# Two batches of the transposed mixer output end to end in one ring tile, so that chunks across a batch border are read in one piece

## Chip, cores and metric

One core of one Trainium2 chip. The metric is the device time of the whole kernel in microseconds (us), lower is better.

## The reference, cut to what matters

A frequency filter mixes each batch along the sequence; a feed-forward part with a leaky ReLU follows, over all tokens.

```python
x: (8, 3008, 256)   w_in: (256, 2048)   w_out: (2048, 256)
y = irfft(rfft(x, axis=1) * (filt_r + 1j * filt_i), n=3008, axis=1)
t = y.reshape(8 * 3008, 256)                # 24064 tokens
h = t @ w_in
out = maximum(0.01 * h, h) @ w_out
```

24064 tokens are 47 chunks of 512. A batch has 3008 tokens, 5.875 chunks, so each of the 7 inner batch borders falls inside a chunk.

## The kernel before

The mixer writes each batch, transposed, into one of two tiles in turn (channels on partitions, tokens along the row, two halves `dt` of 128 channels). The first product of the feed-forward part reads chunks of 512 tokens from there.

```python
yts = [cpool.tile([P, NDT, N], FP16, name=f"yt{i}") for i in range(2)]
...
def sb_group(b, g, copy):                     # last step of the mixer
    dt, h = g // 8, g % 8
    def go():
        ...                                   # 4 matmuls into a PSUM bank
        yv = yts[b % 2][:, dt, :].rearrange("p (a c) -> p a c", c=N2)
        copy(yv[:, :, ds(4 * h, 4)], ps.rearrange("p c a -> p a c"))     # L246
    return go
...
def moe1_group(ci, g):                        # first product of chunk ci, 8 groups
    ...
    pieces, t = [], ci * CH
    while t < (ci + 1) * CH:                  # cut at every batch border
        e = min((ci + 1) * CH, (t // N + 1) * N)
        pieces.append((t // N, t % N, t - ci * CH, e - t))
        t = e
    for j in range(2):
        ct = 2 * g + j
        for b, lo, o, ln in pieces:
            for dt in range(NDT):
                nc.tensor.matmul(ph[:, j, ds(o, ln)], w_in_sb[:, dt, ts(ct, P)],   # L376
                                 yts[b % 2][:, dt, ds(lo, ln)],
                                 start=(dt == 0), stop=(dt == NDT - 1))
    nc.scalar.activation(gts[ci][:, ds(2 * g, 2), :], ph, AF.Lrelu)      # L381

def moe2_slice(ci, g):                        # second product, 8 matmuls of 256 columns: L390
    ...
    nc.scalar.copy(ost[:, tj % 2, :], po)     # every second slice: L397
...
for slot in range(SL * (NCHUNK + 1)):         # a chunk is 8 slots
    ci, g = divmod(slot, SL)
    if ci < NCHUNK:
        moe1_group(ci, g)
    for f in tasks.get(slot, ()):             # steps of the mixer for a later batch
        f()
    if ci > 0:
        moe2_slice(ci - 1, g)
```

Ahead of the slots stands a start of some 42 us: warm-up matmuls, the loads, and the mixer of batch 0. From the first matmul of L376 on I call it the main stage.

## Time and profile before

| | before |
|---|---|
| whole run, 3 runs | 783.31 us median (783.25 to 783.39) |
| span of the profiled run | 782.1 us (a fourth run, of 783.91 us) |
| TensorE busy | 99% |
| start, up to the first matmul of L376 | 42.48 us |
| matmuls of L376 | 1728 |

The page gives each engine's busy time, the chain of waits and the groups of instructions. The lines are in the prediction.

### The profile page before, as it was taken

What the parts mean: (1) busy time and instruction counts of PE and PEld (TensorE: products, weight loads), DVE (VectorE), ACT (ScalarE), POOL (GpSimd) and SP (SyncE); (2) the same over time, 40 slices, a digit from 0 to 9 for tenths busy, and PEclk for the clock granted to TensorE, in tenths of its full rate; (3) what the DMA queues carried; (4) which work ended last, traced back from release to release, by engine and by line L of the source; (5) the groups of instructions that cost most, each with busy time, mean ns of one, the idle gap of its engine ahead of it and who ended that gap; (6) DMA issues with size and microseconds to landing.
All of it is one profiled execution on the core that took longest, in us unless ns stands there. A gap on an engine that the chain in (4) does not pass through costs nothing.

```text
span 782.1 us, 13672 instructions
## 1 busy us (share of the span) xinstructions
PE 773.4 (99%) x5844; PEld 531.4 (68%) x5844; DVE 367.3 (47%) x462; ACT 551.2 (70%) x784; POOL 152.3 (19%) x126
## 2 busy tenths in 40 slices
PE   9899999999999999999999999999999999999998
PEld 4366677666776667766777667776677666776666
DVE  3879751865237641577307754087432765200000
ACT  3686769676787767777587775967668776666664
POOL 5963300340004300052001510025000340000000
PEclk9999999999999999999999999999999999999999
DMA  9963102301041101510105010140101001101111
GB/s 179 226 110 73 38 28 56 94 27 42 28 108 41 41 28 41 108 42 28 42 28 121 28 37 32 42 107 28 41 28 41 28 28 41 41 33 35 41 41 54
DMA packets 39387, 44.16 MB, mean 56 GB/s; under 512 B 11266, under 2 KB 37506, under 8 KB 38658
## 3 DMA queue, kind: packets, MB, share of 16 engines
q0 software_dynamic: 13136, 17.78, 13.3%
q1 hardware_dynamic: 26192, 25.53, 9.3%
q8 instruction: 45, 0.74, 0.4%
q14 instruction: 14, 0.11, 0.0%
HBM read 35.67 MB, written 24.64 MB: 77 GB/s over the span
## 4 chain that ended last, share of the span: by engine, by line
PE 94%; DMA 2%; POOL 2%; ACT 1%; DVE 1%; issue 1%; POOLq 0%
PE ph L376 41%; PE po_ps L390 41%; PE pf L176 3%; PE pf L243 2%; PE pf L231 2%; PE pf L216 2%; DMA fb_sb<-in_filt_i_dram 2%; PE pf L390 1%; POOL fy_h_c L276 1%; ACT big L187 0%; POOL x_sb L132 0%; DVE big L297 0%; ACT big L290 0%; POOL fb_sb L140 0%; ACT gt_c L381 0%
## 5 line engine op out<-in xcount | busy, mean ns | idle before, releaser
L381 ACT ACTIVATE gt_c<-ph 128x1024 f16<-128x1024 f32 x376 | 384.8, 1023 | 195.7 <-PE ph L376 194.7
L376 PE MATMUL ph<-yt,w_in_sb 128*128 128x512 f16 (+7 forms) x1728 | 386.7, 351 | 0.3
L390 PE MATMUL po_ps<-w_out_sb,gt_c 128*128 128x256 f16 x2944 | 381.4, 272 | 0.6 <-ACT ost_c_t L397 0.6
L390 PEld LDWEIGHTS <-gt_c 128*128 128x128 f16 x3008 | 290.7, 98 | 87.1 <-issue 1.9
L376 PEld LDWEIGHTS <-w_in_sb 128*128 128x128 f16 x1728 | 162.9, 98 | 94.4 <-issue 0.4
L224 POOL TENSOR_TENSOR y_b_g<-p_b_g,p_b_g 128x512 f16<-128x512 f32 x84 | 106.9, 1272 | 225.4 <-DVE p_b_g L222 225.4
L199 DVE STREAM_TRANSPOSE big<-big 128x1024 f32<-128x1024 f32 x32 | 55.9, 1847 | 126.2 <-ACT big L187 126.2
L187 ACT CAST big<-pf 128x512 f16<-128x512 f32 x186 | 106.6, 604 | 1.7 <-PE pf L256 1.7
L246 DVE CAST yt<-pf 128x376 f16<-128x376 f32 x112 | 56.3, 544 | 86.0 <-PE pf L243 86.0
L220 DVE TENSOR_TENSOR p_b_g<-pf,fa_sb 128x512 f32<-128x512 f32 x84 | 58.1, 692 | 38.1 <-PE pf L216 35.6
L397 ACT COPY ost_c_t<-po_ps 128x256 f32<-128x256 f32 x184 | 69.4, 377 | 6.6 <-PE po_ps L390 5.4
L207 DVE STREAM_TRANSPOSE big<-big 128x1024 f32<-128x1024 f32 x28 | 51.1, 1934 | 34.1 <-ACT big L187 34.1
L221 DVE TENSOR_TENSOR p_b_g<-pf,fb_sb 64x512 f32<-64x512 f32 x84 | 58.2, 692 | 1.1
L222 DVE TENSOR_TENSOR p_b_g<-pf,fb_sb 64x512 f32<-64x512 f32 x84 | 57.4, 683 | 1.1
L132 POOL DMA_DIRECT2D x_sb<-in_x_dram x12 | 6.6, 553 | 253.3 <-PE pf L176 252.5
L243 PEld LDWEIGHTS <-big 128*128 128x128 f16 x448 | 25.6, 98 | 13.2
L176 PE MATMUL pf<-x_sb,f_sb 94*128 94x256 f16 x224 | 33.9, 272 | 0.2 <-DVE yt L246 0.2
L231 PE MATMUL pf<-y_b_g,small_sb 128*128 128x512 f16 x84 | 31.8, 379 | 0.0
L216 PE MATMUL pf<-big,small_sb 128*128 128x512 f16 x84 | 31.8, 379 | 0.0
L243 PE MATMUL pf<-i_sb,big 128*128 128x94 f16 x448 | 28.6, 206 | 0.0
L176 PEld LDWEIGHTS <-f_sb 94*128 94x128 f16 x224 | 20.9, 97 | 9.1 <-issue 0.4
L318 PE MATMUL po_ps<-idle 128*128 128x512 f16 x72 | 19.5, 418 | 1.2 <-DVE one L165 1.2
(46 smaller groups left out, 158.8 us busy)
## 6 DMA issues: line engine op xcount, KB each, us to landing
out_dram<-ost_c_t SPq DMA_DIRECT2D x92, 256.0 KB, 2.1
x_sb<-in_x_dram POOLq DMA_DIRECT2D x6, 1536.0 KB, 11.4
x_sb<-in_x_dram POOLq DMA_DIRECT2D x3, 480.0 KB, 9.8
fa_sb<-in_filt_r_dram POOLq DMA_DIRECT2D x6, 192.0 KB, 10.2
fb_sb<-in_filt_i_dram POOLq DMA_DIRECT2D x6, 192.0 KB, 8.5
w_in_sb<-in_moe_w_in_dram POOLq DMA_DIRECT2D x1, 1024.0 KB, 13.0
w_out_sb<-in_moe_w_out_dram POOLq DMA_DIRECT2D x1, 1024.0 KB, 13.0
x_sb<-in_x_dram POOLq DMA_DIRECT2D x1, 1024.0 KB, 7.9
```

The costliest lines, as they stand in the source:

```text
L176: nc.tensor.matmul(ps[:, j, :], f1_sb[:N1, n2, :], x_sb[:N1, n2, :], start=True, stop=True)
L187: copy(paired(dst)[:, ds(n0, nn), ds(e0, de)], ps.rearrange("p n (e t) -> p n e t", t=2))
L220: nc.vector.tensor_tensor(p1[:], ps, fa, AL.mult)
L221: nc.vector.tensor_tensor(p2[0:64], ps[64:P], fb[64:P], AL.mult)
L222: nc.vector.tensor_tensor(p2[64:P], ps[0:64], fb[0:64], AL.mult)
L224: nc.gpsimd.tensor_tensor(y1[:], p1[:], p2[:], AL.add)
L243: nc.tensor.matmul(ps[:, j, :], src[:, dt, n2, :], i1_sb[:, n2, :], start=True, stop=True)
L246: copy(yv[:, :, ds(4 * h, 4)], ps.rearrange("p c a -> p a c"))
L376: nc.tensor.matmul(ph[:, j, ds(o, ln)], w_in_sb[:, dt, ts(ct, P)], yts[b % 2][:, dt, ds(lo, ln)], start=(dt == 0), stop=(dt == NDT - 1),)
L381: nc.scalar.activation(gts[ci][:, ds(2 * g, 2), :], ph, AF.Lrelu)
L390: nc.tensor.matmul(po, gts[ci][:, ct, ts(tj, P)], w_out_sb[:, ct, :], start=(ct == 0), stop=(ct == NCT - 1))
L397: nc.scalar.copy(ost[:, tj % 2, :], po)
```

## The change

Intent: the two tiles become the halves of one tile of twice the length. A border between an even batch and the odd one after it then has its tokens side by side, and the chunk across it needs one piece. Only where the ring wraps (borders 2, 4 and 6) does a chunk stay cut.

```diff
-    yts = [cpool.tile([P, NDT, N], FP16, name=f"yt{i}") for i in range(2)]
+    yt = cpool.tile([P, NDT, 2 * N], FP16, name="yt")
...
-            yv = yts[b % 2][:, dt, :].rearrange("p (a c) -> p a c", c=N2)
+            yv = yt[:, dt, ds((b % 2) * N, N)].rearrange("p (a c) -> p a c", c=N2)
...
-            e = min((ci + 1) * CH, (t // N + 1) * N)
-            pieces.append((t // N, t % N, t - ci * CH, e - t))
+            e = min((ci + 1) * CH, (t // (2 * N) + 1) * 2 * N)
+            pieces.append((t % (2 * N), t - ci * CH, e - t))
...
-            for b, lo, o, ln in pieces:
+            for lo, o, ln in pieces:
...
-                        yts[b % 2][:, dt, ds(lo, ln)],
+                        yt[:, dt, ds(lo, ln)],
```

(The copy of the first batch is changed like that of the others.)

More of the change, by code (lines that the diff above doesn't have):

```diff
@@ L307, in first_sb @@
                                  i1_sb[:, n2, :], start=True, stop=True)
-        yv = yts[0][:, dt, :].rearrange("p (a c) -> p a c", c=N2)
+        yv = yt[:, dt, :N].rearrange("p (a c) -> p a c", c=N2)
         copy(yv[:, :, ds(4 * h, 4)], ps.rearrange("p c a -> p a c"))
```

## The prediction

> **What bounds the kernel now.** I read the page first: engines, slices, and the chain that ended last. In the fence: busy time by engine, then the slices of TensorE and its granted clock, then the chain by engine.
>
> ```profile
> PE 773.4 (99%) x5844; PEld 531.4 (68%) x5844; DVE 367.3 (47%) x462; ACT 551.2 (70%) x784; POOL 152.3 (19%) x126
> ...
> PE   9899999999999999999999999999999999999998
> ...
> PEclk9999999999999999999999999999999999999999
> ...
> PE 94%; DMA 2%; POOL 2%; ACT 1%; DVE 1%; issue 1%; POOLq 0%
> ```
>
> TensorE is busy in every slice, at full clock, and is 94% of the chain of waits. All that the other engines do from about 42 us on lies beside it. Second, the waits of TensorE over the whole span (us in total, times, longest): if it waited anywhere in the main stage, the change could add to that or take from it.
>
> ```profile
> PE po_ps L390 <- ACT ost_c_t L397: 0.6, 3, 0.2
> PE pf L176 <- DVE yt L246: 0.2, 1, 0.2
> ```
>
> These are the only two rows from the main stage (the six others are waits of the first 43 us); together under 1 us. So the time of the main stage is the number of columns that TensorE streams, plus what each instruction costs beside its columns. Third, the groups by shape give the matmuls that the change touches: columns after the x, count, busy time, mean.
>
> ```profile
> L376 PE MATMUL ph<-yt,w_in_sb 128*128 128x512 f16 x1280 | 328.7, 379 | 0.3
> ...
> L376 PE MATMUL ph<-yt,w_in_sb 128*128 128x448 f16 x64 | 15.7, 353 | 0.0
> ...
> L376 PE MATMUL ph<-yt,w_in_sb 128*128 128x64 f16 x64 | 7.1, 193 | 0.0
> ```
>
> The reader could take 193 ns for the price of a 64-column matmul and 379 for a 512-column one, and find that a split into 448 and 64 costs 353 + 193 - 379 = 167 ns. That is the trap here: these are latencies of overlapping instructions. What counts is from start to start. So fourth, I took stretches of three whole chunks from the end of the run, where the mixer has finished and TensorE does nothing but the two products of the feed-forward part. Chunk 41 (the middle one) holds the border of batches 6 and 7; its neighbours hold none. First all instructions, then those of L376 alone (width of stretch, then busy us and count of each engine).
>
> ```profile
> 674.15:688.04 13.89, 13.89 (x98) 9.39 (x96) 0.00 (x0) 9.24 (x13) 0.00 (x0) 1.00 0.11 38
> 688.04:702.01 13.97, 13.97 (x130) 10.32 (x128) 0.00 (x0) 9.24 (x13) 0.00 (x0) 1.00 0.11 39
> 702.01:715.91 13.90, 13.90 (x98) 9.39 (x96) 0.00 (x0) 9.25 (x13) 0.00 (x0) 1.00 0.11 39
> ```
>
> ```profile
> 674.15:688.04 13.89, 8.21 (x32) 3.13 (x32) 1.00 0.11 38
> 688.04:702.01 13.97, 8.29 (x64) 4.06 (x64) 1.00 0.11 39
> 702.01:715.91 13.90, 8.21 (x32) 3.13 (x32) 1.00 0.11 39
> ```
>
> This is the change measured inside the kernel before: 64 matmuls and 64 weight loads in place of 32 and 32, for the same columns, last 13.97 instead of 13.89 us. The price of a split chunk is 0.08 us, or 0.08 / 32 = 2.5 ns per added matmul with its weight load.
>
> **What the Trainium skill says.** "TensorE: Matmul & The Clock Gate", section "Wait — 56ns, not 53.3ns?", gives start to start of warm matmuls as N / 2.4 GHz plus a fixed cost of about 2.5 ns, with a floor near 25 ns. The trace agrees: an unsplit chunk is 32 matmuls of 512 columns and 64 of 256, so 32 x 215.8 + 64 x 109.2 = 13.89 us, the first row; and the extra 2.5 ns per matmul is the step to the second. I read the single starts too: 189.1 ns after a 448-column matmul, 28.8 after a 64-column one, 215.8 after 512; the pair is 217.9. The narrowest piece is still over the floor.
> The same page, section "Back-to-back issue gap", says of sustained pairs of weight load and matmul that 512 columns take about 131 ns and 128 about 81. The trace disagrees (215.8, and 55.8 after a 128-column piece), and the measurement decides; taking 81 for 128 would make the splits look dear.
> Section "LDWEIGHTS (loading the stationary operand)" there has P / 1.2, 107 ns for 128 columns. The trace shows 98 ns for one load, yet 64-column matmuls, each with its own load, start 28.8 ns apart. So loads are hidden even there, and removing 128 of them gives nothing further.
> "Perfetto Trace Analysis", section "Identifying the Most-Contended Engine", warns that matmul busy time is a poor measure since matmuls are pipelined. It agrees: mean duration 379 ns at a spacing of 215.8.
>
> **The change part by part.**
> Removed: batches are 3008 tokens and chunks 512, so each of the 7 inner borders falls inside a chunk (5, 11, 17, 23, 29, 35, 41), at column 448, 384, 320, 256, 192, 128, 64. Each such chunk has 8 groups x 2 tiles x 2 pieces x 2 halves = 64 matmuls, not 32; 40 x 32 + 7 x 64 = 1728, the count on the page. In the ring, batches 0-1, 2-3, 4-5 and 6-7 lie end to end. The borders inside a pair (chunks 5, 17, 29, 41) are read in one piece. Those between pairs (11, 23, 35), where the ring wraps, stay split. So 4 x 32 = 128 matmuls and 128 weight loads go: 1728 to 1600. The built programs agree: 256 instructions fewer on TensorE, the same number on every other engine.
> Price: 4 x 0.08 = 0.32 us for all four. For chunks 17 and 29 (320 + 192) the starts give 135.8 + 82.6 = 218.4, 2.6 ns over 215.8, so the same 0.08 us.
> Added: nothing. The ring takes the place of two tiles of the same total size; the copies into it keep their shape and step; the matmul reads 512 neighbouring columns.
> Moved: the waits. One tile instead of two could make writes to one half wait for reads of the other. I traced each semaphore wait in the two built programs to the instruction it waits for: of 2,594 waiting places (the matmuls of one product taken together) none differs. Only the place inside the border product changes: the first matmul now needs the copies of the later batch, where the second piece did.
> On the path: all 0.32 us, since TensorE is the path in these chunks. Sum: 783.31 - 0.32 = 782.99, say **783.0 us**, a gain of 0.04%.
>
> **The rivals.**
> 1. *The merged read waits for the mixer.* Only border 1 is near: its last copy into the tile and the first product of chunk 5 are these rows (start, duration).
>
> ```profile
> 115.95 1.00 DVE L246 CAST yt<-pf 128x376 f16<-128x376 f32 x2 [1.08 <-PE pf L243]
> ...
> 117.65 1.04 PE L376 MATMUL ph<-yt,w_in_sb 128*128 128x448 f16 x8
> ```
>
> The copy ends at 116.95, 0.7 us before the product, and the merge brings the need forward by at most two 448-column starts, 0.38 us, at one place. At the other borders the slack is 7 us and more. Cost 0; if I am wrong, 0.1 to 0.3 us once, and the gain shrinks to nothing.
> 2. *ScalarE becomes the bound in three of the four chunks.* Chunks 5, 17 and 29 also carry the first stage of a later batch, and ScalarE is busy 15.79 of 17.05 us in chunk 5. Its copy out of the output bank ends 142 to 155 ns before TensorE's next write there; where TensorE does wait on it (at 94.05 and 227.35 us, say), the distance is 52, so about 90 are spare. ScalarE starts each activation when a product ends, so the lead doesn't add up: a product is only 4 x 2.5 = 10 ns shorter, and 90 goes to about 80. For it: ScalarE is nearly full. Against: the margin holds level from slot to slot. If it won, only chunk 41's 0.08 us would stay: 783.2.
> 3. *Writes serialise against reads in the one tile.* A copy would then sit between products in each of 56 mixer slots; at perhaps 0.5 us (my estimate, from the copy's 0.54) that is some 28 us, slower by 3.6%. The equal waits of the two programs rule it out.
> 4. *The split costs its latency.* 128 x 167 ns = 21 us, faster by 2.7%. The 0.08 us of chunk 41 rules it out.
>
> **Range and chances.** The three runs before lie within 0.14 us. The candidates left are 783.0 (expected), 783.2 and 783.3 (gain eaten), plus the scatter of a different build in the first 43 us, where TensorE does wait, for which I allow 0.3 us: 782.6 to 783.4. Either 2% bound is 15.7 us away and would need rival 3 or 4. Within 2%: 0.99; 0.005 on each side.
>
> **What would show it.** Right: L376 at 1600 matmuls, 1408 of them of 512 columns, 64 each of 384, 256 and 128, none of 448, 320, 192 or 64; chunk 41 at 13.89 to 13.90 us and L376 in it at 8.21; TensorE still 99% busy; its waits still these two rows and under 1 us. Wrong: a row in which L376 or L390 waits for VectorE or ScalarE in chunks 5, 17 or 29; chunk 41 unchanged at 13.97 with half the matmuls (the 2.5 ns would then not be a cost per instruction); or the copies of L246 starting later with respect to their matmuls.

## The result, and the profile after

783.37 us median of 6 runs (783.10 to 784.10), against 783.35 us for 6 runs of the kernel before (783.18 to 783.98). The ratio is 1.0001, with a 95% interval from 0.9988 to 1.0014. A ratio is the mean time of one kernel's fast runs over that of the other's of the same rounds, so it is not quite the ratio of the medians. In whole runs the forecast gain of 0.32 us is not there.

In the trace it is. First, busy time by engine on the page of the changed kernel, then its groups of L376 by shape (shape, count, busy us, mean ns):

```profile
PE 772.2 (99%) x5716; PEld 524.0 (67%) x5716; DVE 367.4 (47%) x462; ACT 551.0 (71%) x784; POOL 152.2 (19%) x126
```

```profile
L376 PE MATMUL ph<-yt,w_in_sb 128*128 128x512 f16 x1408 | 361.5, 379 | 0.3
L376 PE MATMUL ph<-yt,w_in_sb 128*128 128x384 f16 x64 | 14.8, 326 | 0.0
L376 PE MATMUL ph<-yt,w_in_sb 128*128 128x128 f16 x64 | 8.8, 219 | 0.0
L376 PE MATMUL ph<-yt,w_in_sb 128*128 128x256 f16 x64 | 8.3, 273 | 0.0
```

There are 128 matmuls and 128 weight loads fewer, 1600 of L376 in all, and only borders 2, 4 and 6 still show as pieces. Next, the stretches of chunks 40, 41 and 42 of the changed kernel (its chunk 41 runs from 687.32 to 701.21 us), all engines, with the same columns as in the prediction:

```profile
673.43:687.32 13.89, 13.89 (x99) 9.39 (x97) 0.00 (x0) 9.24 (x13) 0.00 (x0) 1.00 0.11 39
687.32:701.21 13.89, 13.89 (x99) 9.38 (x96) 0.00 (x0) 9.24 (x13) 0.00 (x0) 1.00 0.11 38
701.21:715.11 13.90, 13.90 (x99) 9.40 (x97) 0.00 (x0) 9.25 (x13) 0.00 (x0) 1.00 0.11 39
```

Chunk 41 is now like its neighbours, 13.89 us where it was 13.97. From the starts in the two traces, each merged chunk lost the same 0.080 us: chunk 5 went from 17.054 to 16.974, chunk 17 from 16.173 to 16.093, chunk 29 from 15.293 to 15.213, chunk 41 from 13.973 to 13.893. The waits of TensorE in the main stage are the same two as before:

```profile
PE po_ps L390 <- ACT ost_c_t L397: 0.5, 3, 0.2
PE pf L176 <- DVE yt L246: 0.2, 1, 0.2
```

And the copy that border 1 waits for has kept its distance: it ends at 116.51 us, and the product begins 0.68 us later.

```profile
115.50 1.01 DVE L246 CAST yt<-pf 128x376 f16<-128x376 f32 x2 [1.08 <-PE pf L243]
...
117.19 1.03 PE L376 MATMUL ph<-yt,w_in_sb 128*128 128x512 f16 x4
```

So the question is why a gain that stands in the trace to 0.01 us does not stand in the time.

### The profile page after: what moved, and what is told of

Read it like the earlier page. It is cut to its first block, busy times and chain, and to the rows that moved or that the text cites. A ratio compares the mean times of both kernels' runs of the same rounds, so it can differ in the third digit from the quotient of the medians.

```text
span 781.3 us, 13416 instructions
## 1 busy us (share of the span) xinstructions
PE 772.2 (99%) x5716; PEld 524.0 (67%) x5716; DVE 367.4 (47%) x462; ACT 551.0 (71%) x784; POOL 152.2 (19%) x126
## 4 chain that ended last, share of the span: by engine, by line
PE 94%; DMA 2%; POOL 1%; ACT 1%; DVE 1%; issue 1%; POOLq 0%
PE ph L376 41%; PE po_ps L390 41%; PE pf L176 3%; PE pf L243 2%; PE pf L231 2%; PE pf L216 2%; DMA x_sb<-in_x_dram 1%; DMA fa_sb<-in_filt_r_dram 1%; PE pf L390 1%; POOL fy_h_c L276 1%; ACT big L187 0%; DVE big L297 0%; ACT big L290 0%; ACT gt_c L381 0%; PE ph L306 0%
## 5 line engine op out<-in xcount | busy, mean ns | idle before, releaser
L376 PE MATMUL ph<-yt,w_in_sb 128*128 128x512 f16 (+3 forms) x1600 | 386.4, 366 | 0.3
L376 PEld LDWEIGHTS <-w_in_sb 128*128 128x128 f16 x1600 | 154.5, 98 | 95.7 <-issue 0.4
```

## The experiments

**Theory 1**: the gain is real and on the path, and the whole-run medians hide it, because the start varies by more than it from run to run. **Rival**: the main stage itself varies, or what is won in it is given back elsewhere. In all, 12 runs were made, of ten different kernels, on three chips, each with runs of the kernel before beside it. All results were correct.

### The changed kernel again, and the kernel before against itself

No edit, 5 rounds each.

> The changed kernel, unaltered. Theory 1 (the gain is real and all on the path, 0.08 us in each of four chunks, and only the scatter of the start hides it): from the first product of L376 to the end 739.2 to 739.4 us again, as in its first profile (739.27; before 739.63), chunks 5, 17, 29 and 41 again 0.08 us shorter than before, while the start before it differs from the 42.0 us of the first profile by tenths; ratio to before 0.9996, inside an interval that holds 1. Theory 2 (the main stage itself moves by tenths from run to run, and the 0.36 us between the first two profiles is chance): the stretch from the first product to the end comes out anywhere between 739 and 740, and the start repeats.

> The kernel before, unaltered, timed against itself: what the timing can resolve. Theory 1: from the first product of L376 to the end 739.6 to 739.7 us again, the start off from 42.5 by tenths; the ratio differs from 1 by up to 0.0005, as much as the whole gain of 0.32 us (0.0004). Theory 2: the main stage is off from 739.63 by tenths.

Measured: the changed kernel 783.04 us median (782.44 to 783.94), ratio 0.9997 (0.9984 to 1.0009). The kernel before against itself: 783.27 us (782.92 to 783.38), ratio 0.9998 (0.9986 to 1.0011). The runs of before beside them went from 782.56 to 784.11, which is five times the gain.

The next three fences are the order in time of TensorE's work in three traces (start, duration, in brackets the idle time before): before, before again, changed. Each has the first stage on the second of four parts of x, the first product of the main stage, and the second product of the last chunk.

```profile
12.59 0.38 PE L256 MATMUL pf<-x_sb,f_sb 94*128 94x256 f16 x2 [0.42 <-DMA x_sb<-in_x_dram]
...
42.48 0.87 PE L376 MATMUL ph<-yt,w_in_sb 128*128 128x512 f16 x2
...
771.48 7.15 PE L390 MATMUL pf<-w_out_sb,gt_c 128*128 128x256 f16 x64
```

```profile
11.55 0.38 PE L256 MATMUL pf<-x_sb,f_sb 94*128 94x256 f16 x2
...
41.49 1.32 PE L376 MATMUL ph<-yt,w_in_sb 128*128 128x512 f16 x4
...
770.52 7.15 PE L390 MATMUL pf<-w_out_sb,gt_c 128*128 128x256 f16 x64
```

```profile
11.76 0.38 PE L256 MATMUL pf<-x_sb,f_sb 94*128 94x256 f16 x2 [0.59 <-DMA x_sb<-in_x_dram]
...
42.02 1.31 PE L376 MATMUL ph<-yt,w_in_sb 128*128 128x512 f16 x4
...
770.68 7.15 PE L390 MATMUL pf<-w_out_sb,gt_c 128*128 128x256 f16 x64
```

Subtract the second row from the third: 729.00 and 729.03 us for the same program in two runs, 728.66 for the changed one (728.66 and 728.65 in two more traces of it). The main stage repeats within 0.03 us, and the change takes 0.36 off it. The start of the very same program differs by 0.99 us (42.48 and 41.49). The difference is there when TensorE comes to the second part of x: at 12.59 us, after 0.42 us of waiting for its load, or at 11.55 without a wait. The loads of the first two parts had landed 8.5 and 10.6 us after their issue in the one trace, 7.4 and 9.6 in the other. From the second part to the first product both take 29.9 us. (The changed kernel's trace takes 30.3 there, with 0.4 us more of waiting for GpSimd, so the loads are not all of it.) So the second run of the kernel *before* has a shorter span, 781.1 us, than the first of the changed one, 781.3.

What follows the main stage repeats too: from the second product of the last chunk to the end of the span it is 10.61 to 10.63 us in all five traces of these two kernels, and the time of a run is 1.7 to 1.9 us over its span wherever both are on record. So in these traces the rival falls: what varies is the start, and nothing is given back behind the main stage. (One trace below has a longer main stage.)

### The ring alone, the start held back

To shrink the start's scatter I let VectorE fill the tile of the first stage seven times, so that the loads of x have long landed when that stage may begin. Four kernels got this: before, changed, a ring that is still cut at every border, and the longer ring below. The edit, and that of the ring that is cut:

```diff
+    for _ in range(7):
+        nc.vector.memset(big[0][:], 0.0)
...
-    keep_warm(28)
+    keep_warm(28 + 75)
```

```diff
 # changed kernel, cut as before
-            e = min((ci + 1) * CH, (t // (2 * N) + 1) * 2 * N)
+            e = min((ci + 1) * CH, (t // N + 1) * N)
```

> The kernel before with the start held back: VectorE first fills the tile of the first stage 7 times (some 3.6 us each by my estimate, from 0.91 us for a quarter of that size), so that the first stage cannot begin before about 27 us, when the loads of x have long landed; 75 more warm-up matmuls keep TensorE busy meanwhile. Theory 1 (the whole-run scatter comes from the landing of the first loads, about 1 us from run to run): about 14 to 18 us more in all, and its runs agree within 0.3 us in place of 1.5; main stage 739.6 again. Rival (the scatter is in the tail or the launch): the runs still spread over 1 us or more.

> The changed kernel with the start held back in the same way. Theory 1: its runs agree within 0.3 us, and their mean is 0.3 to 0.4 us under that of the held kernel before, now visible in whole runs. Rival (the gain in the main stage is given back outside of it): no difference of the means, or one under 0.1 us.

> The ring tile alone: held start, copies into the ring, but pieces still cut at all seven borders as before (1728 matmuls of L376). If the removed matmuls are the cause, it equals the held kernel before within 0.1 us, and chunks 5, 17, 29 and 41 take 17.05, 16.17, 15.29 and 13.97 us; if the layout itself does something (reads or writes at other addresses), it is off by more.

> The ring of 12 chunks, no split at all, held start. By its first profile (main stage to the last product 0.54 us under before, 0.17 under the changed kernel): 0.5 to 0.6 us under the held kernel before and 0.15 to 0.2 under the held changed one.

The first product and the second product of the last chunk in the traces of the held kernel before, then of the held changed one:

```profile
66.01 1.32 PE L378 MATMUL ph<-yt,w_in_sb 128*128 128x512 f16 x4
...
795.03 7.15 PE L392 MATMUL pf<-w_out_sb,gt_c 128*128 128x256 f16 x64
```

```profile
65.80 1.31 PE L378 MATMUL ph<-yt,w_in_sb 128*128 128x512 f16 x4
...
794.45 7.15 PE L392 MATMUL pf<-w_out_sb,gt_c 128*128 128x256 f16 x64
```

| start held, one chip | matmuls of L376 | start, us | main stage, us | whole runs, us | mean |
|---|---|---|---|---|---|
| before | 1728 | 66.01 | 729.02 | 806.78 to 807.70 (4) | 807.31 |
| ring, cut at every border | 1728 | 65.93 | 729.81 | 807.16 to 808.00 (4) | 807.56 |
| changed | 1600 | 65.80 | 728.65 | 806.20 to 807.25 (5) | 806.65 |
| ring of 12 chunks | 1504 | 65.93 | 728.47 | 806.17 to 806.73 (4) | 806.48 |

("Main stage" here and below is from the first product to the second product of the last chunk, as in the fences above. The expectations count from the same first product to other ends: 739.27 and 739.63 to the end of the span, 735.81 and 736.15 to the end of the last matmul.) Holding the start cost 24 us, not 14 to 18: a fill took 3.47 us, about as estimated, but each began 0.92 us after the one before it had ended, so that the seven were done at 32.9 us and not at 27.

Three things follow. The start now agrees within 0.21 us over four programs (one trace of each), where it had differed by 0.99 within one and went from 41.28 to 42.48 us over all ten traces with no held start. That is as it should be if the landing of the first loads moved it. The whole runs separate in the expected order: the two kernels with 1728 matmuls average 807.43 over 8 runs, the changed one 806.65, the longer ring 806.48. The rival's second half, that the gain is given back outside the main stage, has no support. But the expected agreement within 0.3 us was missed: the runs of one kernel still spread 0.6 to 1.1 us, and the 0.78 us between 807.43 and 806.65 (standard error 0.23) is over twice the 0.36 of the main stage, so it has luck in it. Against the held kernel before alone, the changed one is 0.66 us faster where 0.3 to 0.4 were expected, and the longer ring 0.83 where 0.5 to 0.6 were, each with a standard error of about 0.25. The changed kernel's 1.05 us is even over the 1 us that the rival named (scatter in the tail or the launch). But the tail is 10.40 to 10.41 us in all four held traces, and time minus span is as steady as before, so the rest of the scatter lies elsewhere in the span. The start is one source and not the only one.

The trace of the ring that is cut shows another source. It was to equal the held kernel before within 0.1 us, and did not: its mean is 0.25 us over, and its main stage is 0.8 us over. All of the 0.8 is one gap in the first chunk, here in the order in time (in brackets the idle time before):

```profile
67.08 0.60 PE L178 MATMUL pf<-x_sb,f_sb 94*128 94x256 f16 x4
...
68.35 1.04 PE L378 MATMUL ph<-yt,w_in_sb 128*128 128x512 f16 x4 [0.68 <-issue]
```

"Issue" says that TensorE waited for nothing that the profile shows. No other trace of a kernel of this size has that gap. It does not seem to come in every run of this kernel: the profiled run, 808.00 us, is the slowest of its four, and the other three average 807.41, against 807.31 for the held kernel before. A fetch of instructions (a transfer of 16 KB) lies close by, from 66.1 to 67.0 us. Other traces tie the two closer: those with pieces of 64 and of 32 columns, below, have nine more gaps of 0.4 to 1.9 us for which the profile names no wait, and each ends 1.2 to 1.5 us after the end of such a fetch, as this one does (1.3). In the other three held traces that fetch was over at the latest 0.1 us after the first product, here 1.1 us after it. This points to a fetch that came late; no run tests it.

The chunks of the ring that is cut answer what it was built for. Its chunks 5, 17, 29 and 41 take 17.053, 16.174, 15.293 and 13.973 us, as before the change: the layout alone saves nothing there, and the removed matmuls are the cause. Chunks 11, 23 and 35 are a hair shorter with the ring, cut or not (16.95, 16.06 and 15.41 us, against 16.96, 16.07 and 15.42). These 0.02 us are the layout's own. They lie in the one wait for ScalarE that each of these chunks has: from start to start, beyond what the columns need, it is 0.344, 0.339 and 0.350 us in the held kernel before, 0.340, 0.334 and 0.342 in the ring that is cut. Why, I do not know.

### The change ten times over, with the sign turned

Every chunk without a border is cut 448 + 64 in the kernel before.

```diff
             e = min((ci + 1) * CH, (t // N + 1) * N)
+            if t == ci * CH and e == t + CH:
+                e = t + 448
```

> The kernel before with every chunk that holds no border split 448 + 64 too: 3008 matmuls of L376 in place of 1728, 1280 more, ten times the change with the sign turned. Theory 1: 1280 x 2.5 ns = 3.2 us more, 786.5, ratio 1.004, with chunks 42 to 44 at 13.97 us each in place of 13.89; a little less if ScalarE is the bound in a part of the mixer's chunks. Rival (such small costs vanish in waits of the main stage): total within 1 us of before.

Measured: 787.02 us median (786.48 to 787.66), ratio 1.0048 (1.0033 to 1.0063). The main stage took 732.15 us, 3.14 over before, and 1280 more matmuls share it: 2.46 ns each. The whole runs show 3.8 us, with the scatter on top. The cost is per instruction and lies on the path. Chunk 42, which holds no border, takes 13.97 us in place of 13.89, as expected (columns as in the prediction's stretches):

```profile
704.60:718.57 13.97, 13.97 (x130) 10.31 (x128) 0.00 (x0) 9.24 (x13) 0.00 (x0) 1.00 0.11 39
```

### How far the 2.5 ns hold

All of L376 in pieces of 64, then of 32 columns.

```diff
-            e = min((ci + 1) * CH, (t // N + 1) * N)
+            e = min((ci + 1) * CH, (t // N + 1) * N, t + 64)      # or 32
```

> The kernel before with all of L376 cut into pieces of 64 columns, 8 to a chunk: 12032 matmuls and weight loads, 10304 more than before. If the price of a piece is a fixed cost per matmul, 2.1 to 2.5 ns, 8 pieces take 230 to 233 ns in place of 215.8 and the total rises by 22 to 26 us, to 805 to 809. If weight loads (98 ns each by the trace) come to bind once no wide piece stands beside the narrow ones, far more: 47 x 32 x 8 x 98 ns alone would be 1179 us.

> The same in pieces of 32 columns, 16 to a chunk. If the fixed cost is all there is, a piece takes 32 / 2.4 + 2.5 = 15.8 ns and 16 of them 253 ns: 56 us over before, 839. If there is a floor of 25 to 29 ns from start to start, as the Trainium skill has it near 25 and as the 28.8 ns of the 64-column piece would allow: 16 x 25 to 29 = 400 to 464 ns, 277 to 373 us over before, 1060 to 1157.

Measured: 811.26 us and 1069.47 us (2 runs each), 27.5 and 285.7 over before. Chunk 42, where the mixer has ended, in the two traces (length of the stretch, then busy us and count of TensorE and of its weight loads), 64 and then 32 columns:

```profile
725.66:740.11 14.45, 14.45 (x322) 13.72 (x320) 0.00 (x0) 9.24 (x13) 0.00 (x0) 1.00 0.12 39
```

```profile
958.37:978.16 19.79, 19.79 (x579) 19.03 (x577) 0.00 (x0) 9.24 (x13) 0.00 (x0) 1.00 0.09 30
```

At 64 columns a chunk has 256 matmuls of L376 in place of 32 and takes 0.56 us longer: 2.5 ns for each of the 224 added, again. The total came 1.5 us over the upper end that was expected. The main stage is 755.53 us, 26.5 over before or 2.6 ns for each added matmul. Two of the gaps told of above, 1.0 us together, are in it, and without them it is 2.5 ns. The other microsecond of the total is of the size of the scatter. At 32 columns the chunk is 5.9 us longer, which is 400 ns for 16 pieces, 25 ns from start to start. That is the floor of the expectation (the near 25 ns of the Trainium skill, "TensorE: Matmul & The Clock Gate", section "Wait — 56ns, not 53.3ns?"), and the fixed cost alone (15.8 ns) is refuted there. Seven of the gaps, 9.7 us together, are in the 285.7 us as well. Each of those matmuls brings its own weight load of 96 ns, so by these durations about four loads are under way at once, and a load does not wait for the end of the one before it. Whether the matmul or its load sets the 25 ns, these runs do not tell apart.

### A ring of 12 chunks, with no cut at all

If the length of the ring is a multiple of the chunk, 6144 columns, no chunk is ever cut. The wrap then falls inside three batches, whose copies are written in two pieces, 48 more copies on VectorE.

```diff
-    yt = cpool.tile([P, NDT, 2 * N], FP16, name="yt")
+    RING = 12 * CH
+    yt = cpool.tile([P, NDT, RING], FP16, name="yt")
...
-            yv = yt[:, dt, ds((b % 2) * N, N)].rearrange("p (a c) -> p a c", c=N2)
-            copy(yv[:, :, ds(4 * h, 4)], ps.rearrange("p c a -> p a c"))
+            yv = yt[:, dt, :].rearrange("p (a c) -> p a c", c=N2)
+            pv = ps.rearrange("p c a -> p a c")
+            a0, a = (b * N % RING) // N2, 0
+            while a < N1:
+                na = min(N1 - a, RING // N2 - (a0 + a) % (RING // N2))
+                copy(yv[:, ds((a0 + a) % (RING // N2), na), ds(4 * h, 4)], pv[:, ds(a, na), :])
+                a += na
...
-        pieces, t = [], ci * CH                   # and the loop that filled it
+        pieces = [(ci * CH % RING, 0, CH)]
```

> The ring lengthened to 12 chunks (6144 columns), so that no chunk is split; three batches are written in two pieces, 48 more copies on VectorE. Matmuls of L376: 1504. Theory 1: chunks 11, 23 and 35 lose up to 0.08 us each as well, though each has one wait of TensorE for ScalarE of about 0.34 us (spacing over what is due), which may grow and eat part: main stage 739.0 to 739.3, total 0.5 us under before. Rival (ScalarE is the bound in these three chunks): they keep 16.95, 16.06 and 15.41 us, their waits grow by as much as the splits cost, and the main stage stays at the changed kernel's 739.27. Theory 2: not to be told from the others.

> The ring of 12 chunks once more: main stage to the last product 735.64 us again; mean of whole runs 0.3 to 0.7 us under before, and 0 to 0.4 under the changed kernel.

> The changed kernel once more, for the whole-run figure. Main stage to the last product 735.81 us again (before 736.15 to 736.18), start anywhere from 41.4 to 42.5. Over all rounds together its mean should come out 0.1 to 0.5 us under that of before; if it is not under it, the gain of the main stage is offset by something outside it that the profiles don't show.

Measured: the ring of 12 chunks 782.96 us (782.47 to 783.15), ratio 0.9993 (0.9981 to 1.0006), and again 782.93 us (782.12 to 784.43), ratio 0.9990 (0.9977 to 1.0003). The changed kernel beside the second: 782.80 us (782.52 to 783.48), ratio 0.9989 (0.9976 to 1.0003). In that second call the expectations on whole runs were missed: the mean of the longer ring was 0.78 us under before (0.3 to 0.7 expected) and 0.03 over the changed kernel's (0 to 0.4 under expected), with one run at 784.43. The main stage of the longer ring is 728.49, 728.47 and, held, 728.47 us: 0.17 to 0.19 under the changed kernel, and not the 0.24 of three more chunks at 0.08. Chunks 11, 23 and 35 lost 0.062, 0.055 and 0.062 us. The rest went into the one wait that each of them has for ScalarE. Here it is in chunk 11, order in time, first the changed kernel, then the longer ring (idle time in brackets):

```profile
226.42 0.10 PEld L390 LDWEIGHTS <-gt_c 128*128 128x128 f16 x1
...
226.81 0.71 PE L390 MATMUL po_ps<-w_out_sb,gt_c 128*128 128x256 f16 x5 [0.18 <-ACT ost_c_t L397]
```

```profile
226.46 0.10 PEld L392 LDWEIGHTS <-gt_c 128*128 128x128 f16 x1
...
227.04 0.81 PE L392 MATMUL po_ps<-w_out_sb,gt_c 128*128 128x256 f16 x6 [0.20 <-ACT ost_c_t L399]
```

TensorE comes to the bank sooner and waits longer for ScalarE's copy out of it: from start to start, beyond what the columns need, 0.358 us in place of 0.340. In these three chunks ScalarE takes about a quarter of the gain. In chunks 5, 17 and 29 it takes nothing: the lead of its copies there fell from 145, 155 and 142 ns to 132, 147 and 135 in chunk 5, and about 52 is where TensorE begins to wait.

### All whole runs together

Without a held start: before 29 runs, mean 783.44 us (782.56 to 784.96); changed 16 runs, mean 783.21 (782.44 to 784.10); ring of 12 chunks 10 runs, mean 782.90 (782.12 to 784.43). The standard deviation of one kernel's runs is 0.5 to 0.65 us, so the 0.23 between the first two has a standard error of 0.16: these runs alone settle neither the sign nor the size, and the gain in whole runs rests on them together with the held ones. They came from several chips; call by call the changed kernel's mean stands at +0.09, -0.16 and -0.81 us from that of before.

## Why the prediction was right or wrong

- *What bounds the kernel; latency against spacing*: right. The 128 matmuls removed were worth 0.080 us for the 32 of each chunk, 2.5 ns each, not the 167 ns that their durations suggest. (The single starts were read a little low: 217.9 for a pair of 448 and 64 columns is 2.1 over 215.8. Over all such pairs in chunks 5 and 41 the starts give 218.2, and the chunk as a whole gives the 2.5.)
- *The change part by part*: right in count (1600, with the shapes named) and price (0.32 us from four chunks, measured 0.320). The main stage fell by 0.36 us; the layout gave 0.02 of the other 0.04, and the rest is a few ns in many places.
- *The waits* (rivals 1 and 2): right, as far as the traces show. No new wait, slack at border 1 unchanged at 0.7 us, ScalarE's lead 7 to 13 ns shorter, where 10 were expected.
- *The rivals 3 and 4*: excluded rightly. The ring cut at every border, where writes and reads share one tile, has no loss near 28 us; 10304 added matmuls cost 26.5 us in the main stage, not 167 ns each.
- *Range and chances*: this is the step that failed. It took "the three runs before lie within 0.14 us" as the scatter and put the gain of 0.32 us on top as 783.0, as if a whole-run median could show it. The median did not fall (783.37 against 783.35). The scatter is what was mis-sized: nine runs of the kernel before spread by 1.55 to 2.26 us within a call, 29 by 2.4 over the calls, with a standard deviation of 0.5. A sign of it: the profiled run of that same kernel took 783.91 us, 0.5 over the slowest of the three. The prediction knew that TensorE waits for loads in the first 43 us, and allowed 0.3 us for it; one unchanged program showed 0.99 us between two runs. That the range of 782.6 to 783.4 holds the median, by 0.03 us, is luck: runs of both kernels lie outside it. Three runs that happen to agree say little about the scatter.
- Still open: the part of the scatter that stays when the start is held, of which one gap of 0.7 us in one trace, with a late fetch of instructions just before it, is all that I have seen.

## What to carry to other kernels

Price a removed instruction by the spacing of starts, best in two stretches of one trace that differ by it alone; here this gave 2.5 ns for a matmul with its weight load, and 0.080 us per chunk to the third digit. It held down to pieces of 64 columns, not at 32. Then compare the gain with the scatter of whole runs, taken from many runs and from the stages that wait for loads, before forecasting that a time will move; a gain of 0.04% must be read in the trace, between two fixed points of the stage that it is in. If a cut is to be avoided altogether, make the ring's length a multiple of the reader's piece and let the writer, whose engine has time, do the cutting.

## What the Trainium skill lacked or had wrong

- "TensorE: Matmul & The Clock Gate", "Back-to-back issue gap": its sustained spacing of about 131 ns for 512 columns and 81 for 128 does not hold here; the runs show 215.8 and 55.8. Its table also has 1 to 64 columns at about 60 cycles (25 ns): 32 columns took 25.0 ns, but 64 took 28.4 to 29.1.
- The same page, "LDWEIGHTS (loading the stationary operand)": it does not say how close loads of new weights may follow each other. With a load before each matmul, starts 25 ns apart were sustained, while each load shows as 96 to 98 ns.
- None of the pages that I read says how much whole executions of one program differ: 782.56 to 784.96 us over 29 runs here, with the second load of x landing 9.6 and 10.6 us after its issue in two traces of one program.
